# Computing the first tiles of h in two row halves, and reordering the first loads, in a fused SiLU-MLP forward and backward kernel

## The chip, the cores and the metric

The kernel runs on one core of one Trainium2 chip. The metric is device time in microseconds (us) of one execution, the lower the better. A ratio in this text is the mean time of one kernel's fast runs over the mean of the other's fast runs of the same rounds, so it is not quite the ratio of the medians that are quoted beside it. All runs of one submission, those of the kernel before among them, were made on one chip; different submissions fell on different chips.

## The reference

```python
# x (1, 2048, 640), w1 (640, 1536), w2 (1536, 640), grad_out (1, 2048, 640), all bf16
def fwd(x, w1, w2):
    h = jnp.einsum("bsd,df->bsf", x, w1)
    return jnp.einsum("bsf,fd->bsd", jax.nn.silu(h), w2)
out, vjp = jax.vjp(fwd, x, w1, w2)
return (out, *vjp(grad_out))          # out, grad x, grad w1, grad w2
```

## The kernel before: the parts that matter

The rows of x are worked off in four chunks of 512 (four tiles of 128 rows each). Only the start of the first chunk changes. Its x tiles are loaded as they lie and transposed on TensorE; w1 is loaded in 128-row tiles ("w1 rows 0" to "4" below are these five tiles), first only their first 512 columns.

```python
    KM = 2; NWARM = 26; NFILL = 4
    # ... 26 matmuls on a constant: they raise TensorE's clock while the first loads are on their way
        load_x_tiles(nc.sync, 0, 1)          # x0          SyncE's queue
        load_x_tiles(nc.scalar, 1, 2)        # x1          ScalarE's queue
        load_x_tiles(nc.sync, 2, STC)        # x2 and x3   one load
        load_w1_rows(nc.scalar, 0, KM)       # w1 rows 0-1
        load_w1_rows(nc.sync, KM, DT)        # w1 rows 2-4
        for fc in range(1, NFC):
            load_w1(fc * FC, (fc + 1) * FC)  # the other 1024 columns of w1
        # ... w2, grad_out
        pe_x_pair(xT_next, 0)                # 10 transposes of x0, x1, and 5 copies from PSUM
        for i in range(NFILL):
            nc.tensor.matmul(wp[:, 0:P], lhsT=warm, rhs=warm, start=True, stop=True)
        pe_x_pair(xT_next, 2)                # the same for x2, x3

        def h_first(xT, aT, ghT):
            # ... hps: four PSUM banks of 128 x 512
            for dt_ in range(KM):
                for ft in range(FB):
                    h_mm(hps[ft], ft, xT, dt_, dt_ + 1)   # 8 matmuls of 512 columns (rows of x)
            # ... then rows 2-4 of w1, and the eight other groups of h
```

The four fill matmuls depend on nothing, and in the instruction stream they stand directly behind the 26 warm-up matmuls.

## Time and profile before

| | kernel before |
|---|---|
| time, three runs | 321.52 to 321.60 us, median 321.60 |
| span of the profiled run | 319.7 us |
| TensorE busy | 315.5 us |
| TensorE without a break from | 5.9 us to the end |

From the profile page of the kernel before: the span, and the busy time of each engine with its share of the span and its instructions (PE is TensorE, PEld its weight loads, DVE VectorE, ACT ScalarE).

```profile
span 319.7 us, 3584 instructions
...
PE 315.5 (99%) x1506; PEld 146.0 (46%) x1506; DVE 101.5 (32%) x181; ACT 77.5 (24%) x142; POOL 0.7 (0%) x6
```

The chain of waits of the kernel before (start us, length us, what it was):

```profile
1.19 3.96 DMA x_nat<-in_x_dram
5.93 13.05 PE hp L158 x60
18.98 12.95 PE hp L221 x60
```

So after 5.9 us nothing but matmuls decides the time. Whatever the change wins or loses must lie before.

The timeline of the kernel before, of TensorE and the first issues (start us, length us, engine, line, operation, output<-input, count; in brackets the idle time before and what ended it; SPq and ACTq are the queues of SyncE and ScalarE):

```profile
0.77 2.93 PE L98 MATMUL wp<-const-bfloat16-1.0 128*128 128x128 bf16 x26 [0.77 <-PEq L385]
1.17 0.47 ACTq L127 DMA_DIRECT2D w_nat<-in_w_dram  x1
1.66 0.46 SPq L127 DMA_DIRECT2D w_nat<-in_w_dram  x1
...
3.50 0.52 PE L153 MATMUL wp<-const-bfloat16-1.0 128*128 128x128 bf16 x4
3.85 0.72 PE L147 MATMUL tp<-ident,x_nat 128*128 128x128 bf16 x10
...
5.20 0.73 PE L147 MATMUL tp<-ident,x_nat 128*128 128x128 bf16 x10 [0.62 <-DMA x_nat<-in_x_dram]
5.87 10.30 PE L158 MATMUL hp<-xT,w_nat 128*128 128x512 bf16 x47
```

Such lines also tell the clock. Twenty-six warm-up matmuls take 2.93 us; the last one counts 0.31, the other 25 steps are 105 ns each, in the trace 107 but for the first. Ten transposes of the same size take 0.72 us; without the last one's 0.22 that is 56 ns a step. The clock has doubled in between, in this trace at 3.8 us. (Single steps below are differences of matmul starts in the trace.)

The loads (output<-input, queue, count, size, us from issue to landing), from the DMA view of the kernel before; with the issue times above, x2 and x3 land at 5.2 us, w1 rows 0-1 at 5.5, w1 rows 2-4 at 6.8:

```profile
w_nat<-in_w_dram SPq DMA_DIRECT2D x1, 384.0 KB, 5.2
x_nat<-in_x_dram SPq DMA_DIRECT2D x1, 320.0 KB, 4.0
w_nat<-in_w_dram ACTq DMA_DIRECT2D x1, 256.0 KB, 4.3
```

And two half microseconds of the kernel before (stretch in us, its length; then PE, PEld, DVE, ACT, POOL busy; granted clock; mean busy share of the DMA engines; GB/s). The trace records only the changes of the granted clock, and the view counts a stretch before the first recorded change as 1.00, so below the steps between matmuls tell the clock:

```profile
4.50:5.00 0.50, 0.08 (x2) 0.00 (x0) 0.41 (x2) 0.43 (x2) 0.00 (x0) 1.00 1.08 372
5.00:5.50 0.50, 0.30 (x6) 0.30 (x7) 0.00 (x0) 0.00 (x0) 0.00 (x0) 1.00 1.03 348
```

### The profile page before, as it was taken

What the parts mean: (1) busy time and instruction counts of PE and PEld (TensorE: products, weight loads), DVE (VectorE), ACT (ScalarE), POOL (GpSimd) and SP (SyncE); (2) the same over time, 40 slices, a digit from 0 to 9 for tenths busy, and PEclk for the clock granted to TensorE, in tenths of its full rate; (3) what the DMA queues carried; (4) which work ended last, traced back from release to release, by engine and by line L of the source; (5) the groups of instructions that cost most, each with busy time, mean ns of one, the idle gap of its engine ahead of it and who ended that gap; (6) DMA issues with size and microseconds to landing.
All of it is one profiled execution on the core that took longest, in us unless ns stands there. A gap on an engine that the chain in (4) does not pass through costs nothing.

```text
span 319.7 us, 3584 instructions
## 1 busy us (share of the span) xinstructions
PE 315.5 (99%) x1506; PEld 146.0 (46%) x1506; DVE 101.5 (32%) x181; ACT 77.5 (24%) x142; POOL 0.7 (0%) x6
## 2 busy tenths in 40 slices
PE   8999999999999999999999999999999999999996
PEld 6444444444444444444444444444444444444443
DVE  1771541477510087710147741000000100001101
ACT  3960000545201254411064520110100001001100
POOL 0000000000000000000000000000000000000000
PEclk9999999999999999999999999999999999999999
DMA  7999999999689887392544079809999999996211
GB/s 259 333 201 203 240 262 254 328 274 310 183 218 331 200 236 125 127 308 76 133 146 139 2 260 267 214 22 296 261 240 258 239 194 319 232 302 186 82 43 41
DMA packets 147040, 66.69 MB, mean 209 GB/s; under 512 B 112592, under 2 KB 147024, under 8 KB 147024
## 3 DMA queue, kind: packets, MB, share of 16 engines
q1 hardware_dynamic: 146608, 66.03, 80.3%
q10 hardware_dynamic: 416, 0.43, 0.4%
q8 instruction: 12, 0.20, 0.3%
q14 instruction: 4, 0.03, 0.0%
HBM read 9.18 MB, written 28.97 MB: 119 GB/s over the span
## 4 chain that ended last, share of the span: by engine, by line
PE 98%; DMA 1%; SPq 0%; DVE 0%; issue 0%; DVEq 0%
PE hp L221 32%; PE hp L158 16%; PE hp L309 16%; PE hp L205 16%; PE hp L357 15%; DMA x_nat<-in_x_dram 1%; PE hp L339 1%; PE tp L147 0%; SPq L124 0%; DVE g L350 0%; DVEq L350 0%
## 5 line engine op out<-in xcount | busy, mean ns | idle before, releaser
L205 PE MATMUL hp<-goT,w2T 128*128 128x512 bf16 x240 | 56.9, 379 | 0.0
L158 PE MATMUL hp<-xT,w_nat 128*128 128x512 bf16 x240 | 56.9, 379 | 0.0
L221 PE MATMUL hp<-aT,w_nat 128*128 128x512 bf16 x240 | 52.5, 379 | 0.0
L221 PE MATMUL hp<-ghT,w1T 128*128 128x512 bf16 x240 | 52.5, 379 | 0.0
L309 PE MATMUL hp<-a_blk,go_nat 128*128 128x512 bf16 x240 | 52.0, 379 | 0.0
L357 PE MATMUL hp<-gh_blk,x_nat 128*128 128x512 bf16 x224 | 48.5, 379 | 0.0
L229 ACT ACTIVATE oT<-hp 128x512 bf16<-128x512 f32 x24 | 14.3, 597 | 109.8 <-PE hp L221 109.8
L167 ACT ACTIVATE aT<-hp 128x512 bf16<-128x512 f32 x48 | 30.0, 627 | 32.6 <-PE hp L158 32.6
L221 PEld LDWEIGHTS <-w1T 128*128 128x128 bf16 x240 | 23.5, 98 | 28.3
L205 PEld LDWEIGHTS <-w2T 128*128 128x128 bf16 x240 | 23.5, 98 | 28.3
L309 PEld LDWEIGHTS <-go_nat 128*128 128x128 bf16 x240 | 23.5, 98 | 28.3
L221 PEld LDWEIGHTS <-w_nat 128*128 128x128 bf16 x240 | 23.4, 98 | 28.4
L158 PEld LDWEIGHTS <-w_nat 128*128 128x128 bf16 x240 | 23.5, 98 | 28.1
L231 DVE CAST oT<-hp 128x512 bf16<-128x512 f32 x16 | 11.1, 691 | 77.0 <-PE hp L221 77.0
L212 DVE SCALAR_TENSOR_TENSOR ghT<-ghT,hp 128x512 bf16<-128x512 bf16 x48 | 32.5, 681 | 7.3 <-PE hp L205 7.3
L357 PEld LDWEIGHTS <-x_nat 128*128 128x128 bf16 x224 | 21.9, 98 | 26.4
L174 DVE SCALAR_TENSOR_TENSOR ghT<-aT,v 128x512 bf16<-128x512 bf16 x48 | 32.8, 686 | 0.5
L171 ACT ACTIVATE t<-hp 128x512 f32<-128x512 f32 x48 | 29.9, 628 | 0.0
L173 DVE TENSOR_SCALAR v<-t 128x512 bf16<-128x512 f32 x48 | 20.2, 425 | 30.3 <-ACT t L171 30.3
L368 DVE CAST g<-hp 128x512 bf16<-128x512 f32 x7 | 4.8, 692 | 47.0 <-PE hp L357 25.8
L319 DVE CAST g2T<-hp 128x512 bf16<-128x512 f32 x7 | 4.8, 691 | 46.1 <-PE hp L309 46.1
L317 ACT ACTIVATE g2T<-hp 128x512 bf16<-128x512 f32 x8 | 4.8, 597 | 47.0 <-PE hp L309 47.0
(21 smaller groups left out, 25.5 us busy)
## 6 DMA issues: line engine op xcount, KB each, us to landing
aT_scr<-aT SPq DMA_DIRECT2D x4, 1536.0 KB, 6.6
ghT_scr<-ghT SPq DMA_DIRECT2D x4, 1536.0 KB, 8.0
out_dram<-o_sb SPq DMA_DIRECT2D x8, 640.0 KB, 3.3
oT_scr<-oT SPq DMA_DIRECT2D x4, 640.0 KB, 3.9
go_nat<-in_grad_out_dram SPq DMA_DIRECT2D x4, 640.0 KB, 8.1
gxT_scr<-oT SPq DMA_DIRECT2D x4, 640.0 KB, 4.7
w_nat<-in_w_dram SPq DMA_DIRECT2D x1, 1920.0 KB, 13.4
x_nat<-in_x_dram SPq DMA_DIRECT2D x3, 640.0 KB, 8.1
```

The lines of the kernel that those rows point to most:

```text
L158: nc.tensor.matmul(hp[:], lhsT=w1_nat[:, dt_, ft * P:(ft + 1) * P], rhs=xT[:, dt_, :], start=(dt_ == 0), stop=(dt_ == DT - 1),)
L167: nc.scalar.activation(aT[:, ft, :], hp[:], ACT.Silu)
L171: nc.scalar.activation(t[:], hp[:], ACT.Tanh, scale=0.5)
L173: nc.vector.tensor_scalar(out=v[:], in0=t[:], scalar1=-0.5, scalar2=0.5, op0=ALU.mult, op1=ALU.add)
L174: nc.vector.scalar_tensor_tensor(out=ghT[:, ft, :], in0=aT[:, ft, :], scalar=1.0, in1=v[:], op0=ALU.subtract, op1=ALU.mult)
L205: nc.tensor.matmul(gp[:], lhsT=w2T[:, dt_, ft * P:(ft + 1) * P], rhs=goT[:, dt_, :], start=(dt_ == 0), stop=(dt_ == DT - 1),)
L212: nc.vector.scalar_tensor_tensor(out=ghT[:, ft, :], in0=ghT[:, ft, :], scalar=1.0, in1=gp[:], op0=ALU.add, op1=ALU.mult)
L221: nc.tensor.matmul(op_[:], lhsT=w_all[:, ft, dt_ * P:(dt_ + 1) * P], rhs=rhs_all[:, ft, :], start=(ft == 0), stop=(ft == FT - 1),)
L229: nc.scalar.activation(oT[:, dt_, :], op_[:], ACT.Copy)
L231: nc.vector.tensor_copy(out=oT[:, dt_, :], in_=op_[:])
L309: nc.tensor.matmul(gp[:], lhsT=go_nat[:, st, dt_ * P:(dt_ + 1) * P], rhs=a_blk[:, st, :], start=(st == 0), stop=(st == ST - 1),)
L357: nc.tensor.matmul(gp[:], lhsT=x_nat[:, st, dt_ * P:(dt_ + 1) * P], rhs=gh_blk[:, st, :], start=(st == 0), stop=(st == ST - 1),)
```

## The change

Between the two sets of transposes TensorE is idle for about 0.6 us. The change wants to fill that gap with real work: the first eight matmuls of h, which need w1 rows 0-1, are cut into a left half (the rows of x0 and x1) and a right half (x2 and x3). Six left halves run before the second transposes. For this w1 rows 0-1 must come earlier: they go behind x0 on SyncE's queue, x3 goes behind x1 on ScalarE's, x2 behind w1 rows 0-1. Two fill matmuls are dropped.

```diff
+    NTAIL = 2
-    NFILL = 4
+    NFILL = 2
         load_x_tiles(nc.sync, 0, 1)
         load_x_tiles(nc.scalar, 1, 2)
-        load_x_tiles(nc.sync, 2, STC)
-        load_w1_rows(nc.scalar, 0, KM)
+        load_w1_rows(nc.sync, 0, KM)
+        load_x_tiles(nc.scalar, 3, STC)
+        load_x_tiles(nc.sync, 2, 3)
         load_w1_rows(nc.sync, KM, DT)
         # ... (the second transposes share four PSUM banks instead of five, and move into h_first)
-        pe_x_pair(xT_next, 2)
         def h_first(xT, aT, ghT):
+            left, right = slice(0, SC // 2), slice(SC // 2, SC)
+            for k in range(KM * FB):
+                if k == KM * FB - NTAIL:
+                    pe_x_pair(xT, 2, tps)
+                h_mm(hps[k % FB], k % FB, xT, k // FB, k // FB + 1, left)
             for dt_ in range(KM):
                 for ft in range(FB):
-                    h_mm(hps[ft], ft, xT, dt_, dt_ + 1)
+                    h_mm(hps[ft], ft, xT, dt_, dt_ + 1, right, start=False)
```

More of the change, by code (lines that the diff above doesn't have):

```diff
@@ L141, with x_banks, pe_x_pair, h_mm @@
         nc.sync.dma_start_transpose(out=w1T[:], in_=w1[:, :])
-        def pe_x_pair(xT, st):
-            for dt_ in range(DT):
-                tp = ps_h.tile([P, 2, P], dt_in, name="tp", tag="hp")
-                for q in range(2):
-                    nc.tensor.transpose(tp[:, q, :], x_nat[:, st + q, dt_ * P:(dt_ + 1) * P], ident[:])
-                copy = nc.scalar.copy if dt_ % 2 else nc.vector.tensor_copy
-                copy(out=xT[:, dt_, st * P:(st + 2) * P], in_=tp[:])
-        pe_x_pair(xT_next, 0)
+        def x_banks(groups):
+            tps = []
+            for g in groups:
+                tps.append((g, ps_h.tile([P, len(g), 2, P], dt_in, name="tp", tag="hp")))
+            return tps
+        def pe_x_pair(xT, st, tps):
+            for k, (g, tp) in enumerate(tps):
+                for i, dt_ in enumerate(g):
+                    for q in range(2):
+                        nc.tensor.transpose(
+                            tp[:, i, q, :], x_nat[:, st + q, dt_ * P:(dt_ + 1) * P], ident[:]
+                        )
+                copy = nc.scalar.copy if k % 2 else nc.vector.tensor_copy
+                for i, dt_ in enumerate(g):
+                    copy(out=xT[:, dt_, st * P:(st + 2) * P], in_=tp[:, i].rearrange("p q r -> p (q r)"))
+        pe_x_pair(xT_next, 0, x_banks([(dt_,) for dt_ in range(DT)]))
         for i in range(NFILL):
             nc.tensor.matmul(wp[:, 0:P], lhsT=warm, rhs=warm, start=True, stop=True)
-        pe_x_pair(xT_next, 2)
-        def h_mm(hp, ft, xT, lo, hi):
+        def h_mm(hp, ft, xT, lo, hi, cols=None, start=True):
+            cols = cols or slice(0, SC)
             for dt_ in range(lo, hi):
                 nc.tensor.matmul(
-                    hp[:],
+                    hp[:, cols],
                     lhsT=w1_nat[:, dt_, ft * P:(ft + 1) * P],
-                    rhs=xT[:, dt_, :],
-                    start=(dt_ == 0),
+                    rhs=xT[:, dt_, cols],
+                    start=(start and dt_ == 0),
                     stop=(dt_ == DT - 1),
+                    skip_group_check=True,
                 )
@@ L184, in h_first @@
         def h_first(xT, aT, ghT):
+            tps = x_banks([(0,), (1,), (2, 3), (4,)])
             hps = []
```

## The prediction

> **What bounds the kernel now.** TensorE. The table of busy time gives PE 315.5 of 319.7 us, and the chain of waits is an unbroken row of matmuls from 5.93 us on. A 512-column matmul follows its predecessor by 216 ns (timeline). The change can only win what lies before 5.9 us. There the timeline shows: warm-up matmuls to 3.8, ten transposes of x tiles 0 and 1 at 3.85, PE idle, ten transposes of x tiles 2 and 3 at 5.20, first h matmul at 5.87. The chain names the load of x tiles 2 and 3 (issue 1.19, landing 5.16). Other landings (DMA view): x0 3.64, x1 3.83, w1 rows 0-1 on ScalarE's queue 5.47, w1 rows 2-4 6.86.
>
> **What the change does.**
> 1. Eight of the first 512-column matmuls become 16 of 256 columns; six left halves run before the second transposes. No 256-column matmul is in the trace; between 56 ns (128 columns, measured) and 216 ns (512) the line gives an estimate of 109 ns, which "TensorE: Matmul & The Clock Gate", section Back-to-back issue gap, gives too. Six halves, 0.65 us, move into idle time: the ceiling.
> 2. For that, w1 rows 0-1 must land early, and x tile 2 goes behind them. The loads get no faster: "DMA: Bandwidth & Descriptors", section Issuing engines are not separate DMA queues, says both queues share the same 16 engines; the trace agrees (about 370 GB/s in total from 3 to 5 us, both queues active). From the packet records, on the slowest engine x0 and x1 end at 3.44 us; a 1280-byte packet takes 55 ns, a 1024-byte one 46. A tile of x is 8 packets per engine, w1 rows 0-1 are 16. Estimates: w1 rows 0-1, sharing with x3, end at 4.6 and land (0.4 us later, as measured for the loads of before) at 5.0, half a microsecond earlier than now; x2 ends at 5.07, lands at 5.45, 0.3 us LATER than now. w1 rows 2-4 still land at about 6.9.
> 3. Two fill matmuls fewer: no effect.
> 4. Transposed copies: same number and size; the first end at 4.91, before the halves start.
>
> **Sum.** Halves 5.03 to 5.69 (they end after x2's landing, so they set the start), transposes 0.67, two left and eight right halves 1.09: the remaining h matmuls start at 7.45. Before: 5.87 + 8 x 0.216 = 7.60. [...] Of the ceiling of 0.65 us I expect 0.1 to 0.3 to survive, because the halves start late (w1) and x2 is later. Everything after shifts by that and keeps its length.
>
> **Predicted time: 321.35 us, range 321.0 to 321.7.** Faster by over 2%: 0.005; within 2%: 0.99; slower by over 2%: 0.005.
>
> **What would show each step.** Right: six 256-column matmuls 109 ns apart between 5.0 and 5.7; second transposes starting at 5.5 to 5.7; x2 landing after 5.3; w1 rows 0-1 landing at 4.8 to 5.1; no PE idle after the second transposes; the next stage starting 0.1 to 0.3 us before 18.98. Wrong: halves waiting for copies or PSUM banks; a wait for w1 rows 2-4 at about 7 us.
>
> **What would make it wrong.** If the queues share unequally and w1 rows 0-1 land at 4.7, the gain is 0.4 to 0.6 us. If w1 lands at 5.3 or later, or the second copies delay the right halves, or the clock of TensorE (the warm-up steps from 107 to 56 ns at 3.8 us) rises later with fewer fills, there is no gain or a small loss. A large effect in later stages would contradict the unbroken row of matmuls.

## The result

The changed kernel took 321.73 to 321.93 us, median 321.82, over four runs; the kernel before, in the same rounds, 321.52 to 321.92, median 321.60. The ratio of the fast runs is 1.0005 with a 95% interval of 0.9988 to 1.0023. By the rule of 2% that is the same time; but the predicted gain of 0.25 us did not come, and the time lies above the predicted range of 321.0 to 321.7. Later the unchanged changed kernel gave medians of 322.00 against 321.62 and 322.25 against 321.92. Of its 14 runs, 12 lie above the median of the kernel before on the same chip, by 0.17 to 0.24 us in the means. So what has to be explained is a lost gain of a quarter of a microsecond and probably a loss of about 0.2.

The profile after, the same views. The page:

```profile
span 320.0 us, 3570 instructions
...
PE 314.8 (98%) x1483; PEld 147.2 (46%) x1512; DVE 101.7 (32%) x181; ACT 77.6 (24%) x142; POOL 0.7 (0%) x6
```

The matmul count is short of the 1512 weight loads because some matmul records are missing from this trace; the busy time of TensorE is that much too small and is not used below. The timeline of the changed kernel:

```profile
1.20 0.43 SPq L128 DMA_DIRECT2D w_nat<-in_w_dram  x1
1.68 0.47 SPq L125 DMA_DIRECT2D x_nat<-in_x_dram  x1
2.19 0.43 SPq L128 DMA_DIRECT2D w_nat<-in_w_dram  x1
...
3.50 0.42 PE L164 MATMUL wp<-const-bfloat16-1.0 128*128 128x128 bf16 x2
...
3.84 1.25 PE L155 MATMUL tp<-ident,x_nat 128*128 128x128 bf16 x10
...
5.00 1.37 PE L169 MATMUL hp<-xT,w_nat 128*128 128x256 bf16 x6
6.18 0.57 PEld L155 LDWEIGHTS <-x_nat 128*128 128x128 bf16 x10 [0.20 <-DMA x_nat<-in_x_dram]
6.21 0.72 PE L155 MATMUL tp<-ident,x_nat 128*128 128x128 bf16 x10
...
6.77 9.46 PE L169 MATMUL hp<-xT,w_nat 128*128 128x256 bf16 x47
```

Its loads of w1 rows 0-1, of x2, and of w1 rows 2-4, and the two half microseconds:

```profile
w_nat<-in_w_dram SPq DMA_DIRECT2D x1, 256.0 KB, 3.8
x_nat<-in_x_dram SPq DMA_DIRECT2D x1, 160.0 KB, 4.5
...
w_nat<-in_w_dram SPq DMA_DIRECT2D x1, 384.0 KB, 5.1
```

```profile
4.50:5.00 0.50, 0.50 (x6) 0.33 (x5) 0.36 (x2) 0.45 (x2) 0.00 (x0) 1.00 0.85 255
5.00:5.50 0.50, 0.50 (x4) 0.38 (x4) 0.29 (x1) 0.29 (x1) 0.00 (x0) 1.00 0.87 235
```

Three things:

1. The ten first transposes take 1.25 us instead of 0.72, and the six halves 1.37 us, 213 ns a step instead of the 109 foreseen. TensorE's clock was still low. It stepped up at 6.2 us, not at 3.8.
2. w1 rows 0-1 landed at 1.20 + 3.8 = 5.0 us as predicted, but x2 at 1.68 + 4.5 = 6.2, not at 5.45. The weight load of the second transposes waited for it until 6.18. A fast clock alone would not have helped here: the transposes could not have started earlier.
3. Between 4.5 and 5.5 us the loads moved at 255 and 235 GB/s, where the kernel before had 372 and 348.

The comparable moment in both kernels is the start of the ninth 512-column step's worth of h: 7.59 us before, 7.86 after. From there to the end of the span are 312.08 us before and 312.15 after. In ten profiles of kernels without a prelude (before, after, e1 to e4, e9, b1, f1, g1; see below) this rest is 312.08 to 312.15 us, so in these everything is decided before it. In the three of p1 and p2 it is longer (312.65, 312.26 and 312.81 us). It is called "the ninth step" from here on.

### The profile page after: what moved, and what is told of

Its sections match the earlier page's. It is cut to its first block, busy times and chain, and to the rows that moved or that the text cites. A ratio compares the mean times of both kernels' runs of the same rounds, so it can differ in the third digit from the quotient of the medians.

```text
span 320.0 us, 3570 instructions
## 1 busy us (share of the span) xinstructions
PE 314.8 (98%) x1483; PEld 147.2 (46%) x1512; DVE 101.7 (32%) x181; ACT 77.6 (24%) x142; POOL 0.7 (0%) x6
## 4 chain that ended last, share of the span: by engine, by line
PE 98%; issue 1%; DVE 0%; DVEq 0%
PE hp L239 32%; PE hp L169 16%; PE hp L223 16%; PE hp L327 16%; PE hp L375 15%; PE hp L357 1%; PE wp L99 1%; PE tp L155 1%; DVE g L368 0%; PE wp L164 0%; DVEq L368 0%
## 5 line engine op out<-in xcount | busy, mean ns | idle before, releaser
L169 PE MATMUL hp<-xT,w_nat 128*128 128x512 bf16 (+1 forms) x241 | 57.2, 375 | 0.4
L169 PEld LDWEIGHTS <-w_nat 128*128 128x128 bf16 x248 | 24.3, 99 | 27.7 <-DMA w_nat<-in_w_dram 0.2
L239 PEld LDWEIGHTS <-w_nat 128*128 128x128 bf16 x240 | 23.5, 98 | 28.3
```

The lines of the kernel that those rows point to most:

```text
L169: nc.tensor.matmul(hp[:, cols], lhsT=w1_nat[:, dt_, ft * P:(ft + 1) * P], rhs=xT[:, dt_, cols], start=(start and dt_ == 0), stop=(dt_ == D ...
L239: nc.tensor.matmul(op_[:], lhsT=w_all[:, ft, dt_ * P:(dt_ + 1) * P], rhs=rhs_all[:, ft, :], start=(ft == 0), stop=(ft == FT - 1),)
```

## The experiments

First theory: the two missing fill matmuls leave a gap of 0.13 us just before the clock would have risen, and that moved the step. Rivals: the step comes at a random moment of its own; or the loads, not the clock, cost the time.

### Fills (e1, e2), a second profile (e3), the old load order (e4)

```diff
 # e1: the changed kernel          # e2: the kernel before       # e3: the changed kernel as it is
-    NFILL = 2                     -    NFILL = 4
+    NFILL = 4                     +    NFILL = 2
```

```diff
 # e4: as e1, and the loads in the order of the kernel before
-        load_w1_rows(nc.sync, 0, KM)
-        load_x_tiles(nc.scalar, 3, STC)
-        load_x_tiles(nc.sync, 2, 3)
+        load_x_tiles(nc.sync, 2, STC)
+        load_w1_rows(nc.scalar, 0, KM)
```

e1: 

> The changed kernel with four fill matmuls again instead of two. Clock theory (the two fills taken away leave TensorE idle for 0.13 us just before its clock would rise, so the rise comes at 6.2 us instead of 3.8): rise back at about 3.8 us, first ten transposes 56 ns apart from 3.85 to 4.4, six half matmuls 109 ns apart from 5.0 to 5.7, first 512-column matmul of h at about 7.45 us (7.86 in the changed kernel), time 321.4 to 321.5, that is 0.3 to 0.4 us less than the changed kernel and 0.1 to 0.2 less than the kernel before. Rival (the fills do not matter; late w1 rows and x tile 2, or copies, cost the time): rise still after 6 us, or a rise at 3.8 without a gain; time 321.8.

e2: 

> The kernel before with two fills instead of four, nothing else. Clock theory: the rise comes at about 6.2 us, all twenty transposes run 107 ns apart, the second ten end at about 6.3 instead of 5.8, first h matmul at 6.3 to 6.4 instead of 5.87; time 321.9 to 322.1, slower by 0.3 to 0.5 us. Rival: rise at 3.8 as before, time 321.6.

e3: 

> The changed kernel unchanged, a second profile of it on this chip. Clock theory: the rise falls at the same 6.2 us again (within 0.1 us), since the same gap precedes it; time 321.8. Rival (the rise comes at a random phase of the run): it falls elsewhere between 3.8 and 7.2 us.

e4: 

> The changed kernel with four fills and the load order of the kernel before (x tiles 2 and 3 together behind x tile 0, w1 rows 0-1 on ScalarE's queue). With the clock back at 3.8 us this shows what the load order is worth: w1 rows 0-1 land at 5.47, halves 5.5 to 6.15, second transposes 6.15 to 6.7, first 512-column matmul at about 7.9; time about 321.9, 0.4 to 0.5 us more than with the new load order. If the load order does not matter: 7.45 us and 321.45.

| five or six runs each, one chip | median us | range us | ratio to before, 95% | clock step in the profile | ninth step |
|---|---|---|---|---|---|
| before (11 runs) | 321.62 | 321.38 to 322.43 | | | |
| e1, changed, 4 fills | 322.01 | 321.43 to 322.31 | 0.9998 to 1.0022 | between 5.0 and 6.1 us | 8.35 |
| e2, before, 2 fills | 321.97 | 321.49 to 322.32 | 0.9999 to 1.0025 | 4.7 us | 7.63 |
| e3, changed again | 322.00 | 321.55 to 322.19 | 0.9996 to 1.0019 | 6.6 us | 8.08 |
| e4, changed, 4 fills, old loads | 322.25 | 321.94 to 324.27 | 1.0008 to 1.0047 | 6.3 us | 8.22 |

The first transposes and what followed, e1 first, then e2:

```profile
3.93 1.27 PE L155 MATMUL tp<-ident,x_nat 128*128 128x128 bf16 x10
6.03 0.83 PE L169 MATMUL hp<-xT,w_nat 128*128 128x256 bf16 x6 [0.83 <-DMA w_nat<-in_w_dram]
```

```profile
3.80 1.17 PE L147 MATMUL tp<-ident,x_nat 128*128 128x128 bf16 x10
5.25 0.73 PE L147 MATMUL tp<-ident,x_nat 128*128 128x128 bf16 x10 [0.27 <-DMA x_nat<-in_x_dram]
```

The first theory fell. With the four fills back (e1) the clock was late again: all ten transposes stepped 107 ns. With two fills (e2) it was early: the last step of the ten is already 56 ns. The kernel before, whose three times had lain within 0.08 us, ran from 321.38 to 322.43 on this chip. The step's moment differs from run to run whatever the kernel does with its fills. The Trainium skill, "TensorE: Matmul & The Clock Gate", section "What's actually happening", gives the reason to expect this: the activity window, about 3.4 us long, runs freely and does not start with the kernel. Over the traces with the 26 warm-up matmuls the readable steps lie from 3.8 to 6.6 us, which agrees with a window of that length.

What the three profiles with the new load order shared was x2: landed at 6.1 us (changed kernel), 6.4 (e1) and 5.9 (e3). In e1 w1 rows 0-1 landed only at 6.0. With the old order x2 and x3 landed at 5.2 (before and e2) and 5.3 (e4). e4 also shows that the halves without their load order have little to run on: w1 rows 0-1 landed at 5.6. Its mean, without the run of 324.27, lies 0.22 us above e1's, less than the 0.4 to 0.5 expected, and its ninth step was even earlier than e1's, so this pair does not show the new order to be better.

### Taking the clock out: two preludes (e5 to e8, then d1 and d2)

To see the change with the clock up, 100 more warm-up matmuls and a barrier of all engines were put ahead of everything, so that no load is issued before the clock has stepped.

```diff
 # e5: the kernel before, e6: the changed kernel
-    NWARM = 26
+    NPRE = 100; NWARM = 45
+        for i in range(NPRE):
+            nc.tensor.matmul(wp[:, 0:P], lhsT=warm, rhs=warm, start=True, stop=True)
+        tc.strict_bb_all_engine_barrier()
 # e7: as e6 with four fills, x2 and x3 in one load
-        load_x_tiles(nc.scalar, 3, STC)
-        load_x_tiles(nc.sync, 2, 3)
+        load_x_tiles(nc.scalar, 2, STC)
 # e8: as e6 with four fills, left halves for all five rows of w1, and w1 ahead of x2 and x3 on both queues
+        load_w1_rows(nc.sync, 0, 1);  load_w1_rows(nc.scalar, 1, 2)
+        load_w1_rows(nc.sync, 2, 3);  load_w1_rows(nc.scalar, 3, DT)
+        load_x_tiles(nc.sync, 2, 3);  load_x_tiles(nc.scalar, 3, STC)
```

e5: 

> The kernel before with 100 more warm-up matmuls and a barrier of all engines ahead of everything, so that no load is issued until TensorE has run for some 8 us; 45 warm-up matmuls instead of 26 after it. Clock theory: the 56 ns step is reached before the first load in every run, so the spread of the times of one kernel (1.05 us over eleven runs of the kernel before on this chip) falls to under 0.5 us, and from the first load on the start repeats the lucky trace of the kernel before: x tiles 2 and 3 land 4.4 us after the first load issue, first h matmul 5.1 us after it. The time itself is some 8 to 10 us longer than the kernel before and counts only against the next three. Rival (the spread comes from elsewhere, landings alone): spread unchanged at about 1 us.

e6: 

> The changed kernel with the same warm prelude. Theory A (clock alone: with the clock up the change would win what was predicted): 0.1 to 0.2 us less than the warm kernel before. Theory B (the new load order makes x tile 2 land 0.7 to 1.0 us later than x tiles 2 and 3 did, which is a second cause of its own): six halves 109 ns apart as soon as w1 rows 0-1 land, then TensorE waits for x tile 2, which lands 5.2 to 5.6 us after the first load issue; time 0.2 to 0.5 us MORE than the warm kernel before.

e7: 

> Changed kernel, warm prelude, but x tiles 2 and 3 in one load on ScalarE's queue behind x tile 1, and w1 rows 0-1, then 2-4, on SyncE's. So both queues have work until the last x tile is in. Theory B1 (with the new order one queue runs dry at about 4 us, and what is left, several short loads one behind the other on one queue, moves at 230 to 260 GB/s instead of 350 to 370): no such dip from the third to the fourth microsecond after the first issue, x tiles 2 and 3 land 4.4 to 4.7 us after it, w1 rows 0-1 at 4.1 to 4.5; time within 0.15 us of the warm kernel before. Rival B2 (w1 rows ahead of x delay it whatever the queues, by their 262 KB): x tiles 2 and 3 land 5.1 us or later and the time stays 0.2 to 0.5 us above the warm kernel before.

e8: 

> Changed kernel, warm prelude, all five row tiles of w1 (first 512 columns) ahead of x tiles 2 and 3, spread over both queues (x0, w1 row 0, row 2, x2 on SyncE's; x1, w1 row 1, rows 3-4, x3 on ScalarE's), and left halves of all five row tiles, 16 before the second transposes and 4 after, then the 20 right halves. If the balance of the queues is what was lost: w1 rows 0 and 1 land 3.8 to 4.0 us after the first issue, rows 2-4 at 4.9, x2 and x3 at 5.7 to 6.0, by when 16 halves are done; the twenty halves replace idle time and the time is 0.3 to 0.5 us less than the warm kernel before. If short loads in series are slow on either queue: no gain, x tiles at 6.3 or later, time 0 to 0.3 us more.

The design had a fault. The barrier waits for the matmuls, and how long 100 of them take depends on when the clock steps; so the step's moment went into the time again. The medians were 330.42, 330.45, 329.96 and 330.32 us, but e5 alone spread from 329.67 to 332.50: the times decide nothing. The profiles can be read from the first load issue on. From there to the ninth step, or the same amount of work (for e8, which by then has done twenty steps' worth, to the 21st) it took 7.33 us in e5, 7.01 in e6, 7.17 in e7; and 10.06 in e8, against 9.92 in e5 to the same point. (Both figures of e5 are worked out: the start of its first h matmul plus 8 or 20 steps of 0.216 us, less the first issue at 8.27 us.) In e6 the changed kernel was thus 0.3 us ahead, although x2 landed 5.3 us after the first issue and TensorE waited for it. e7 helped with the loads: x2 and x3, in one load on the other queue, landed 4.6 us after the first issue, not 5.1 or later, so it is not simply the bytes of w1 rows 0-1 ahead of x that delay it. In e8, with four short loads on either queue, w1 rows 2-4 landed 5.8 to 6.2 us after the first issue instead of 4.9, and the last x tile at 6.9: short loads one behind the other were slow on both queues. I expected the balance of the queues to matter; what e8 showed is that it did not suffice.

A second prelude has a length that TensorE's clock cannot change: three large operations on VectorE set it, and TensorE's 80 matmuls are done before.

```diff
 # d1: the kernel before, d2: the changed kernel
+        nc.vector.memset(hold[:], 0.0)                       # 128 x 2048
+        for i in range(3):
+            nc.vector.scalar_tensor_tensor(out=hold[:], in0=hold[:], scalar=1.0, in1=hold[:],
+                                           op0=ALU.add, op1=ALU.mult)
+        # 80 warm-up matmuls, barrier of all engines, 45 warm-up matmuls
```

d1: 

> The kernel before behind a prelude of fixed length: VectorE works for some 8 us (three large operations), TensorE runs 80 warm-up matmuls meanwhile and is done earlier, a barrier of all engines, then the kernel with 45 warm-up matmuls. In the earlier warm prelude the barrier waited for the matmuls, so the moment of the clock step went into the time again (spread 2.8 us); here it cannot. Clock theory: the spread within this kernel falls to under 0.5 us (0.8 to 1.1 us over the kernels without prelude). First h matmul 5.1 to 5.6 us after the first load issue. Rival (landings alone make the spread): spread about 1 us.

d2: 

> The changed kernel behind the same fixed prelude, on the same chip. Theory A (only the clock spoiled the gain): 0.1 to 0.3 us less than the held kernel before, x tile 2 landing by 4.7 us after the first issue. Theory B (x tile 2 lands 5.0 to 5.7 us after the first issue, because the lone queue crawls): TensorE waits for it after the six halves, and the time is 0.1 to 0.4 us more than the held kernel before.

d1 took 332.65, 330.72, 330.92, 331.20 and 331.07 us, median 331.07. d2 took 330.66, 330.62, 332.40, 330.39, 330.81 and 330.71, median 330.69. Each has one run some 1.5 us above the rest. The rest of d1 spans 0.48 us, the rest of d2 0.42: with the clock held up, most of the spread is gone, as the clock theory said. The slow run of each has a mean granted clock of 0.995, all others 0.999 or 1.000. And here the changed kernel is ahead, by 0.38 us in the medians. Without the slow run of each, the means differ by 0.34 us (95% interval 0.03 to 0.65, from these nine runs) and the ranges overlap by 0.09. The timelines of TensorE, d2 first, then d1 (whose profiled run was its slow one):

```profile
14.30 0.83 PE L180 MATMUL hp<-xT,w_nat 128*128 128x256 bf16 x6 [0.34 <-DVE xT L171]
14.96 0.72 PE L166 MATMUL tp<-ident,x_nat 128*128 128x128 bf16 x10
15.52 3.85 PE L180 MATMUL hp<-xT,w_nat 128*128 128x256 bf16 x21
```

```profile
13.14 0.73 PE L158 MATMUL tp<-ident,x_nat 128*128 128x128 bf16 x10 [1.11 <-DMA x_nat<-in_x_dram]
14.76 1.11 PE L158 MATMUL tp<-ident,x_nat 128*128 128x128 bf16 x10 [0.89 <-DMA x_nat<-in_x_dram]
15.67 2.34 PE L169 MATMUL hp<-xT,w_nat 128*128 128x512 bf16 x5
```

In d2 the six halves take 0.83 us, step 109 ns, and the second transposes follow at once, since behind this prelude x2 landed no later than x2 and x3 did in d1 (5.7 us after the first issue in both). So the idea of the change works where the clock is up and the loads are in time. The start is not quite that of the plain kernel: behind this prelude x0 and x1 landed 3.9 to 4.2 us after the first issue, in the kernel before 2.9 to 3.1. In d1 the matmuls of 512 columns step by 427 ns from 15.7 us on: after two waits of 1.1 and 0.9 us the clock had fallen back. In the trace it is low for 3.4 us (14.95 to 18.36 us); at half rate that costs about 1.7 us, an estimate that covers the 1.5 us of that run.

### A queue that runs dry, or a boundary (e9, b1), and the changed kernel a third time (f1)

Why do the loads crawl between 4.5 and 5.5 us in the changed kernel? The next theory was that ScalarE's queue has run dry by then and a lone queue loses time between two loads. e9 gives it work:

```diff
 # e9: the changed kernel
-        load_w1_rows(nc.sync, KM, DT)
+        load_w1_rows(nc.scalar, KM, DT)
```

e9: 

> The changed kernel (two fills, no prelude) with w1 rows 2-4 moved from SyncE's queue to ScalarE's, behind x tile 3; nothing else. ScalarE's queue then has work while SyncE's goes from w1 rows 0-1 to x tile 2. Theory B1 (a lone queue loses time at the boundary of two loads): the bytes moved by 5.5 us are 1180 to 1220 KB, as with the old order, instead of 1055 to 1087; w1 rows 2-4 land at 6.4 to 6.9 instead of 7.3 to 7.9; x tile 2, which now shares, at 5.7 to 6.0. Rival (the order of the bytes, not the queues): 1050 to 1100 KB by 5.5 us again and w1 rows 2-4 after 7.2. Time within 0.3 us of the changed kernel either way.

e9 took 322.89 us in the median (322.31 to 325.55), against 321.94 for the kernel before. The dip was there all the same, though less deep (277 and 285 GB/s; 1146 KB by 5.5 us, between the two forecasts), x2 landed at 7.2 us and w1 rows 2-4 at 8.7. So a lone queue is not needed for the dip; that it adds to it is not excluded. The next theory was that each boundary between two loads costs something wherever it is. The cleanest test is to cut one load of the kernel before in two and leave the rest alone:

```diff
 # b1: the kernel before
-        load_x_tiles(nc.sync, 2, STC)
+        load_x_tiles(nc.sync, 2, 3)
+        load_x_tiles(nc.sync, 3, STC)
```

b1: 

> The kernel before with the load of x tiles 2 and 3 cut into two loads, one behind the other on the same queue: same bytes, same order, one boundary of two loads more. If a boundary costs (the first packets of a new load take 200 to 700 ns instead of 55): the bytes moved by 5.5 us fall from 1200-1220 KB towards 1100, x tile 3 lands at 5.4 to 5.8 instead of 5.15 to 5.26, time 0.2 to 0.5 us more than the kernel before. If boundaries are free: 5.15 to 5.26, time equal.

The two half microseconds of b1:

```profile
4.50:5.00 0.50, 0.50 (x8) 0.46 (x5) 0.36 (x2) 0.37 (x2) 0.00 (x0) 1.00 0.79 211
5.00:5.50 0.50, 0.18 (x4) 0.05 (x2) 0.39 (x2) 0.37 (x1) 0.00 (x0) 1.00 0.83 267
```

One cut, the same bytes in the same order, and the rate falls from 372 and 348 GB/s to 211 and 267. x3 landed at 5.4 us, w1 rows 2-4 at 7.5 instead of 6.8, and the ninth step came at 7.79 instead of 7.59. On the other queue w1 rows 0-1 landed earlier, at 5.0 instead of 5.5. In the packet records the slow packets (over 150 ns where the median is 55 for a row of x and 46 for a row of w1) number 14 between 3.5 and 5.5 us in b1, and 10 or 11 in the changed kernel, e1, e3 and f1, but 2 to 6 in the four traces with the old loads (before, e2, e4, g1). The times of b1 show less than expected: median 321.93 against 321.92 for the kernel before (mean 0.06 us more), where I had expected 0.2 to 0.5. So in this profile the dip and the late landings came with one load more; that this alone costs time in the kernel before is not shown. It had slack there: w1 rows 2-4, at 7.5, still came ahead of the ninth step. Nor is the dip a law. Of the nine profiles without a prelude that have more loads than the kernel before in the same first bytes (after, e1, e3, f1, b1, e9, p2 and two of p1), eight fell below 290 GB/s in one or both of these half microseconds; the ninth, the second profile of p1 (below), has eight loads instead of five and kept 332 and 348. The four with the old loads stayed at 336 or more.

The packet records also tell how much of a late landing is rate. In e2, e4 and g1, with the old loads, the same number of bytes (1.0 to 2.0 MB) had been moved within 0.1 us of the kernel before; in the three profiles of the changed kernel it took 0.3 to 0.6 us longer, in b1 0.2 to 0.4. The rest of a late landing is then a matter of whose bytes came first.

f1: 

> The changed kernel, third profile of it, and more times on a chip with the others. If the late x tile 2 is part of the change and not an accident: it lands at 5.8 to 6.5 again (6.14 and 5.91 so far, 6.41 with four fills), with a dip to 230-280 GB/s between 4.5 and 5.5 us; the clock step falls somewhere between 3.7 and 7.2; time 0.1 to 0.3 us above the kernel before in the median. If an accident: x tile 2 at 5.3 to 5.6.

f1 is the changed kernel unchanged, third profile. Its median was 322.25 us against 321.92. The timeline of TensorE and the load of w1 rows 2-4, issued at 2.16 us:

```profile
3.80 0.92 PE L155 MATMUL tp<-ident,x_nat 128*128 128x128 bf16 x10
...
5.27 0.83 PE L169 MATMUL hp<-xT,w_nat 128*128 128x256 bf16 x6 [0.55 <-DMA w_nat<-in_w_dram]
5.94 0.72 PE L155 MATMUL tp<-ident,x_nat 128*128 128x128 bf16 x10
6.50 1.26 PE L169 MATMUL hp<-xT,w_nat 128*128 128x256 bf16 x10
8.45 3.84 PE L169 MATMUL hp<-xT,w_nat 128*128 128x512 bf16 x17 [0.70 <-DMA w_nat<-in_w_dram]
```

```profile
w_nat<-in_w_dram SPq DMA_DIRECT2D x1, 384.0 KB, 6.2
```

This run is nearly the prediction's own case: the clock up at 4.2 us, halves 109 ns apart, x2 landed at 5.5 us and in time. But w1 rows 0-1 landed at 5.2 instead of 5.0 and the halves began at 5.27; up to the last right half, at 7.48 us, the row of work was as foreseen but 0.14 us late, so that the ninth step would have come at 7.59, no earlier than in the kernel before. Then TensorE stood still until w1 rows 2-4 landed at 2.16 + 6.2 = 8.4 us, which the prediction had at 6.9. It was the slowest of the three profiles. The rate between 4.5 and 5.5 us was 242 and 174 GB/s. But when w1 rows 2-4 landed, 2.01 MB had been moved, against 1.61 MB in the kernel before at their landing; they and all loads ahead of them hold 1.31 MB. The kernel before had moved 2.01 MB at 7.9 us, so about 0.5 of the 1.6 us by which they were late is rate, and about 1.1 is bytes of later loads that came first. The expectation that x2 itself would be late again missed; the dip came, and the lateness fell on another load.

### What the clock alone costs (g1)

```diff
 # g1: the kernel before
-    NWARM = 26; NFILL = 4
+    NWARM = 1;  NFILL = 0
```

g1: 

> The kernel before with one warm-up matmul instead of 26 and no fills: a direct test of what a late clock step costs. Clock theory: the step cannot come before some 3 us of work from 5.2 us on, so it falls between about 7 and 11 us; all transposes and the first h matmuls run at half rate (107 and 427 ns); time 1 to 3.5 us more than the kernel before. Rival (the step comes at a fixed time whatever TensorE does): step at 3.8 to 7.2, time within 0.5 us.

```profile
3.65 2.65 PE L147 MATMUL tp<-ident,x_nat 128*128 128x128 bf16 x20 [2.61 <-DMA x_nat<-in_x_dram]
6.09 6.26 PE L158 MATMUL hp<-xT,w_nat 128*128 128x512 bf16 x25
```

Here the loads came in time (x2 and x3 at 5.0 us), all transposes stepped 107 ns and the first h matmuls 427 ns, until the clock stepped up at 7.5 us. The ninth step came at 8.5 us. The median was 323.00 us, 1.08 above the kernel before (four runs, 322.41 to 323.76; ratio 1.0027 to 1.0062). A late clock by itself costs a microsecond, several times the predicted gain.

### Two other orders (p1, p2)

Neither cause favours early halves, so I tried whole matmuls with all x tiles first:

```diff
 # p1: the kernel before                              # p2: the kernel before
-        load_x_tiles(nc.sync, 2, STC)                -        load_x_tiles(nc.sync, 2, STC)
-        load_w1_rows(nc.scalar, 0, KM)               -        load_w1_rows(nc.scalar, 0, KM)
-        load_w1_rows(nc.sync, KM, DT)
+        load_x_tiles(nc.sync, 2, 3)                  +        load_x_tiles(nc.sync, 2, 3)
+        load_x_tiles(nc.scalar, 3, STC)              +        load_x_tiles(nc.scalar, 3, STC)
+        load_w1_rows(nc.sync, 0, 1)                  +        load_w1_rows(nc.sync, 0, KM)
+        load_w1_rows(nc.scalar, 1, KM)
+        load_w1_rows(nc.sync, KM, KM + 1)
+        load_w1_rows(nc.scalar, KM + 1, DT)
```

p1: 

> The kernel before (whole 512-column matmuls, four fills) with another load order: x0 and x2 on SyncE's queue, x1 and x3 on ScalarE's, then the w1 rows 0 and 1, one on each, then row 2 and rows 3-4. Both the second transposes and the first h matmul need all of x and w1 rows 0-1, 918 KB either way; if no time is lost at boundaries, x2 and x3 land at 4.7 to 4.9 instead of 5.16, w1 rows 0-1 at 5.4 to 5.6 as before, h starts at 5.5 to 5.6 instead of 5.87; time 0.2 to 0.4 us less than the kernel before. If the shorter loads lose at their boundaries, w1 rows 0-1 land after 5.8 and there is no gain.

p2: 

> The kernel before (whole matmuls) with x3 on ScalarE's queue behind x1, and x0, x2, w1 rows 0-1, w1 rows 2-4 on SyncE's. All x tiles land at 4.3 to 4.6 (4.27 and 4.51 in the earlier run with x first), so both sets of transposes run back to back and TensorE has no gap before 5.1; w1 rows 0-1 land at 5.5 to 5.8; h starts at 5.5 to 5.85 instead of 5.87; w1 rows 2-4 are in time. Time 0.1 to 0.3 us less than the kernel before, and fewer runs above 322.3[...]. If w1 rows 0-1 land after 5.9: no gain.

p1 again: 

> The order with all x tiles first, once more, to see whether it beats the kernel before (first time: medians 321.81 against 321.94, interval 0.9952 to 1.0023, not settled). If it does: 0.1 to 0.4 us less in the median on this chip too, x tiles 2 and 3 at 4.3 to 4.6, h from 5.4 to 5.7. If not: medians within 0.1 us, because w1 rows 1 to 4 and the second column block of w1 then come later and TensorE waits for them between 6 and 10.2 us.

p1 had a median of 321.81 us against 321.94 (ratio 0.9952 to 1.0023) and, on another chip, 322.00 against 321.52 (1.0001 to 1.0028). In its first profile h started at 5.41 us, 0.46 earlier than in the kernel before, and the gain was given back in waits for later parts of w1, the last at 10.1 us. In its second profile (p1 again) the x tiles landed at 4.5 and 4.8 us, but the clock stepped only at 5.2 and w1 rows 0-1 landed at 6.1, so h started at 5.98. It was not shown to beat the kernel before. p2 had a median of 322.32 us (321.38 to 325.08) against 321.92. In its slow profiled run w1 rows 0-1 landed only at 7.7 us, TensorE idled 2 us, and the clock fell back (four of its six runs took 322.3 us or more, against the fewer that were expected); the granted clock (third column from the end) shows it:

```profile
7.00:8.00 1.00, 0.26 (x2) 0.15 (x3) 0.00 (x0) 0.00 (x0) 0.00 (x0) 1.00 1.03 347
8.00:9.00 1.00, 1.00 (x5) 0.42 (x4) 0.00 (x0) 0.00 (x0) 0.00 (x0) 0.72 1.08 377
9.00:12.00 3.00, 3.00 (x8) 1.02 (x7) 0.00 (x0) 0.00 (x0) 0.00 (x0) 0.53 1.08 369
```

No version tried was shown to beat the kernel before.

## Why the prediction was wrong

Its class (within 2%) was right, which says little: only in the first 5.9 of 320 us could anything be won. The time was 0.47 us above the predicted one and outside the range. Point by point, with the three profiles of the changed kernel:

| | predicted | first | e3 | f1 |
|---|---|---|---|---|
| clock step | 3.8, as before | 6.2 | 6.6 | 4.2 |
| w1 rows 0-1 land | 5.0 | 5.0 | 4.9 | 5.2 |
| step between halves, ns | 109 | 213 | 213 | 109 |
| x2 lands | 5.45 | 6.1 | 5.9 | 5.5 |
| w1 rows 2-4 land | 6.9 | 7.3 | 7.9 | 8.4 |
| ninth step | 7.45 | 7.86 | 8.08 | 8.45 |
| limited by | halves | x2, and the clock | the clock | w1 rows 2-4 |

- Right: only what lies before 5.9 us can change, and the rest keeps its length (312.08 to 312.15 us in the ten traces named above). Right: w1 rows 0-1 land at about 5.0. Right: a half takes 109 ns with the clock up (f1, d2), as estimated and as the formula for the isolated gap at full clock gives it in the Trainium skill ("TensorE: Matmul & The Clock Gate", section "Back-to-back issue gap"). Right: copies and PSUM banks did not delay the plain kernels. d1 and d2 show that the idea itself wins, by 0.3 to 0.4 us, where clock and loads allow it.
- Wrong, and the step that failed in the run that was predicted: "x2 ends at 5.07, lands at 5.45", and with it "w1 rows 2-4 still land at about 6.9". They landed at 6.1 and 7.3 there, and up to 8.4 in f1. The sum counted only packets, 55 or 46 ns each, and took the rate of 370 GB/s of the kernel before as given. It had no term for a rate that depends on how the bytes are cut into loads, and none for bytes that overtake. The new order puts one load more into the same bytes, and between 4.5 and 5.5 us the rate fell to 174 to 261 GB/s in all three profiles. b1 shows such a fall with one cut alone. At equal bytes moved this put the changed kernel 0.3 to 0.6 us behind; the rest differs from run to run, and is largest in f1 (1.1 us). That a load more must cost rate is not shown: p1 again did without the dip.
- Wrong, second: the clock. The prediction named a later step among what could go wrong, but only through the dropped fills, and took 3.8 us as the rule. It was the earliest of all the traces with 26 warm-up matmuls. The step's moment changes from run to run, between 3.8 and 6.6 us here, and it hits the changed kernel harder just where the gain should be: six halves at the low clock take 1.2 us up to the next transposes instead of 0.66. "Two fill matmuls fewer: no effect" is neither shown nor refuted: the median of e1 equals that of the changed kernel on the same chip (322.01 and 322.00), that of e2 lies 0.35 us above the kernel before with a ratio interval (0.9999 to 1.0025) that just includes no difference, and the clock steps of their profiles contradict the idea that the fills set it.
- The size: of 0.65 us that could be won, the prediction kept 0.1 to 0.3. It foresaw x2 0.3 us later; 0.7 to 1.0 would have been right in two of three looks.

Open: why the rate falls with more loads, and not in every profile. It is seen as packets of 150 to 730 ns in the changed kernel and a lower rate; whether the engines wait for descriptors, for memory or for earlier writes, no run here tells. Open too is how the loss of about 0.2 us splits between clock and loads, because each profile shows a different limit and the times alone don't tell them apart.

## What to carry to other kernels

A gain of a fraction of a microsecond at the start of a kernel cannot be read from one trace: look at several before you cost it, since both the moment at which TensorE's clock steps up and the landing of each load move by more than the gain. When you cost loads, count the loads and not only the bytes, and leave a margin: in eight of nine profiles here with loads cut smaller the rate dipped, and some of the loads behind landed 1.6 to 2.2 us later than in the kernel before (f1, e9, p2). Before you fill a gap of TensorE with split work, check that what follows the gap is not itself waiting for a load which your reordering has pushed back.

## What the Trainium skill lacked or had wrong

- "DMA: Bandwidth & Descriptors" has no figure for the boundary between two loads on one queue issued by SyncE or ScalarE. Here the rate was 211 and 267 GB/s over a microsecond with one load more and the same bytes, instead of 372 and 348 (b1, one profile); with three loads more it was 332 and 348 in another (p1 again). Its remark in section "Anatomy of one DMA" that the bubble of the semaphore's write is tiny is made for the other path and did not help.
- "TensorE: Matmul & The Clock Gate", section "What's actually happening", has the free-running window (in the clock record of the traces each fall and the rise after it are 3.41 us apart: 8.44 and 11.85 us in p2, 14.95 and 18.36 us in d1). But it gives ±500 ns for the spread of the first step, and here it came between 3.8 and 6.6 us.
- The same section ties the fall of the clock to an idle window of about 3.4 us. Here the clock fell twice at the end of 3.41 us in which TensorE had been idle for only 2.0: in one wait in p2, in waits of 1.1 and 0.9 us in d1. For the rest it had been at work, on transposes and other matmuls. One wait of 1.3 us in d2 did not make it fall.
- The same page puts the warm-up penalty under 1% of a typical kernel and advises against fitting a count of slow matmuls. In g1 it was 0.3% (1.08 of 322 us), true, and still four times the gain that this change was after.
- No page says that a stretch without a clock record reads as full clock in the views: in the changed kernel they show 1.00 from 4.5 to 5.5 us, where the steps of 107 and 213 ns show the low clock, because the record begins with the step at 6.15 us. In p2 the later fall is recorded and reads 0.72 and 0.53.
